# Zero-adding matmuls in TensorE's idle stretches, gate logits by column matmuls, and projections ahead of time in an attention and MLP mix

## The chip, the cores and the metric

The kernel runs on one core of a Trainium2 chip. The metric is device time in microseconds, the median of several runs. TensorE (PE) multiplies, ScalarE (ACT) and VectorE (DVE) work elementwise, GpSimd (POOL) is a slower elementwise engine, and SyncE (SP) issues most DMAs. Each engine takes its own instructions strictly in the order in which they were recorded.

## The reference

Two branches of the same input x (2048 tokens, 512 features, bf16) are mixed by a gate. Attention has 32 heads of 16 features; the other branch is a mixer with two Gelus and two layer norms.

```
x = A_x
g = sigmoid((x * gate_w).sum(-1))
q, k, v = split(x @ wqkv)                  # 32 heads, 16 wide
a = softmax(q k^T / 4) v @ wo
h = gelu(layernorm(x) @ w1)                # 512 wide
hs = shift_tokens(h, by +1, -1, +2, -2 per quarter) @ w2
x1 = x + hs
b = x1 + gelu(layernorm(x1) @ w3) @ w4     # w3: 512 x 1792
out = g * a + (1 - g) * b
```

## The kernel before, in words

**Scores.** Attention goes by rounds: 4 chunks of 512 queries, 4 groups of 8 heads, and two halves of a group, 32 rounds in all. A round has 64 score tiles, each 128 keys by 512 queries of one head: 2048 tiles altogether. A score tile is one matmul (line 800) with 32 rows of the array; up to four run at once in four row strips. Two thirds of the tiles go to ACT, two at a time from a score buffer psA of two PSUM banks (there are two of these), as exact exps (line 880). The others go to DVE, each by way of one of three ring banks: line 906 turns scores into the bits of a number, lines 942 (DVE) and 945 (POOL) make three shifted copies, and the value matmul adds the four up. The value matmuls (line 976) use 17 columns, 16 values and the sum of weights, four heads side by side in the one PSUM bank acc. At a round's end DVE copies acc out (line 992), DMAs and POOL normalise the heads (lines 995 to 1016), with the gate's factor gpk already in it.

**Projections and MLP.** The other products on TensorE are groups of matmuls into a ring bank, four column strips of 32 at once (line 502): q, k and v projections, w1, w2, w3, w4 and the output projection wo. Each is a generator with a planned place `at` (in score tiles issued so far) and a due place. DVE or ACT takes the bank away. There is one Gelu pass for the first MLP (line 693, after w1) and one for each of the four chunks of the second (line 724, between w3 and w4). A pass keeps ACT from its exps, and two loads of its function table lie around it.

**The gate** (lines 598 to 628): sixty-four matmuls, 16 token tiles by 4 pieces of the features, each with 128 x 128 values of x as weights and one column of gate_w moving (line 603). Token logits come out with tokens on partitions; DVE clips them (608), ACT takes the exp, omg = 1 / (1 + exp) is made, and a transpose and DMAs (616 to 627) bring the exps into gpk.

**The order of the work** is made while the program is built. A model of the engines (class Sim) with a cost for each instruction runs through the kernel; whenever it finds TensorE free it calls pe_pick (lines 1129 to 1206). That takes ACT score tiles if a psA buffer is free, DVE tiles if ring banks are free and fewer than DVE_WAIT await DVE, and else, up to the time of the next exp's end, projections (do_gen, from gen_ready) and value matmuls (do_pv). If there is nothing it returns False and TensorE is left idle. All that was emitted is sorted by the model's time and recorded (line 1210). On the chip each engine keeps that order, with semaphores between engines. So a changed constant moves many instructions, and one of TensorE that waits holds back all behind it.

**The end** (lines 1216 to 1262) is written by hand. ACT copies acc; TensorE adds the known part of the last chunk's output projection (`known`, two head groups for each of four token tiles), turns the sums of weights round (line 1237), adds y, the finished other branch (`add_y`), broadcasts the reciprocals (1245) and does the last head group (1255). The four output tiles leave by SP and ACT in turn.

**The start.** Eight zero matmuls (line 480, 512 wide) run while the first inputs load.

Of the kernel before, what the change touches and what calls it, by code (L numbers as in the profile page):

```python
# [233 lines left out]
def kernel(  # L234
# [14 lines left out]
    nc = tc.nc  # L249
# [19 lines left out]
    DVE_STOP = 6  # L269
    DVE_STOP_L = 8  # L270
    URG = 5
    URG_L = 16
    GP3 = 1.0
    DVE_ALONE = 2
    SL = (45, 60)
    IDLE_NS = 544
    FLUSH = 1
    PD_LOW = 0
    PA_LOW = 0
    DVE_WAIT = 2  # L280
    DVE_CAP = 144
    AHEAD = 9
    AHEAD2 = 9
    PV_FULL = 0.92
    PV_IDLE = 0.4
    PRESS = 27
# [7 lines left out]
    P_K = (90, 15)  # L294
    P_V = (8, 6, 6)
    P_V2 = (135, 167)
# [24 lines left out]
    V2 = const.tile([P, NT // 2, H, DH + 1], BF16, name="V2")  # L321
    gw = const.tile([P, KT], BF16, name="gw")
    zero = const.tile([P, 512], BF16, name="zero")
    idb = const.tile([P, P], BF16, name="idb")
# [48 lines left out]
    def dve(hold, deps, fn, **kw):  # L373
        return sim.add(Job("DVE", hold, 150.0, deps, fn, **kw))
# [9 lines left out]

    PSUM_NS = 600.0


# [7 lines left out]
    def W(name):  # L395
        return wb[name].slot
# [41 lines left out]
    dl_w["v1"] = start("SP", 2500.0, col(W("v"), 2 * D + 256, 3 * D))  # L438
    dl_w["g"] = start("SP", 3000.0, lambda q: q.dma_start(out=gw[:], in_=gate_w.rearrange("(kt p) -> p kt", p=P)))
    j_x += [j_x0, j_x1] + [[start("SP", 2500.0, lambda q, c=c: q.dma_start(out=x_sb[:, 4 * c:4 * c + 4, :],  # L440
# [37 lines left out]
    def warm_pe():  # L478
        for _ in range(8):
            nc.tensor.matmul(sim_ring[RING - 1][:], lhsT=zero[:, 0:P], rhs=zero[:], start=True, stop=True)  # L480

# [116 lines left out]
    def gate(at):  # L598
        g = gen("z", at, [dl_w["g"]] + [j_xT[c, 0, k] for c in range(NCH) for k in range(KT)], [])
        units = []  # L600
        for t in range(NT):
            for k in range(KT):
                units.append([Op("full", None, lambda t=t, k=k: nc.tensor.matmul(
                    g.buf.slot[:, t:t + 1], lhsT=W(f"x{t // 4}0")[:, k, (t % 4) * P:(t % 4 + 1) * P], rhs=gw[:, k:k + 1], start=(k == 0),
                    stop=(k == KT - 1)), ns=56.0, name="z")])
        g.units, g.ops = [[o for u in units[i:i + 8] for o in u] for i in range(0, 64, 8)], [o for u in units for o in u]
        g.ops[-1].frees += [wb[f"x{c}0"] for c in range(NCH)]
        e = sim.add(Job("DVE", 120, 150.0, g.ops, lambda: nc.vector.tensor_scalar(
            out=zc[:], in0=g.buf.slot[:, 0:NT], scalar1=60.0, scalar2=-60.0, op0=ALU.min, op1=ALU.max), prio=2,
            frees=[g.buf]))  # L610
        a = act(110, [e], lambda: nc.scalar.activation(out=zE[:], in_=zc[:], func=ACT.Exp))
# [484 lines left out]
    def gen_ready():  # L1096
        if cur_gen[0] is not None:
            return cur_gen[0]
        if not sim.free["ring"]:
            return None  # L1100
        best = None
        for g in gens:
            if g.at <= sim.tiles and (best is None or g.due < best.due) and all(d.done is not None for d in g.deps):
                best = g
        return best
# [23 lines left out]
    def pe_pick():  # L1129
# [71 lines left out]
        if not ops and any(cnt):  # L1201
            do_pv(0.01 if flush else PV_IDLE)
        if not ops:
            return False
        sim.pe_run(ops)
        return True

    sim.run(pe_pick, lambda: acc_round[0] == NR and sim.pending == 0)

    sim.order.sort(key=lambda x: (x[0], x[1]))  # L1210
    if report is not None:
        report.append((sim, [sum(x) for x in n_dve]))
    for _, _, fn in sim.order:
        fn()

# [9 lines left out]
    def known(tt):  # L1225
        for G in range(LG, 4):
            into(tt, lambda a, b: oDbuf[c, G].slot[:, tt * P + a:tt * P + b], lambda: wo[:, G, :], G == LG, False)
# [3 lines left out]

    c = NCH - 1
    nc.scalar.copy(out=ab[:], in_=acc[:])
    known(0)
    known(1)
    for b in range(4):
        nc.tensor.matmul(pd[:, 4 * b:4 * b + 4], lhsT=ab[:, b * P:(b + 1) * P], rhs=idf[:, 0:P:32], start=True, stop=True)
    known(2)
    known(3)
    add_y(1)  # L1240
# [10 lines left out]
    for tt in range(4):  # L1251
        t = NT - 4 + tt
        o = (sim.free["ot"] + sim.free["xn"])[tt]
        for j in range(4):
            nc.tensor.matmul(bank[tt][32 * j:32 * j + 32, :], lhsT=oT[:, tt * P + 32 * j:tt * P + 32 * j + 32], rhs=woL[:],
                             start=False, stop=True, tile_position=(0, 32 * j), skip_group_check=True)
        if tt % 2:
            nc.scalar.activation(out=o[:], in_=bank[tt], func=ACT.Copy, scale=omg[:, t:t + 1])
        else:
            nc.vector.scalar_tensor_tensor(out=o[:], in0=bank[tt], scalar=omg[:, t:t + 1], in1=y_of(tt), op0=ALU.mult,  # L1260
                                           op1=ALU.add)
        (nc.scalar if tt % 2 else nc.sync).dma_start(out=out_flat[t * P:(t + 1) * P, :], in_=o[:])

# [28 lines left out]
```

## Time and profile before

| what | number |
|---|---|
| median of 7 runs | 795.58 us (795.23 to 798.81) |
| the profiled execution's own time | 798.81 us |
| its span, first to last instruction | 797.0 us |
| mean granted TensorE clock | 0.983 |
| exps of ACT, L880 | 737, 1038 ns each, 691.4 us |
| DVE's first step, L906 | 574, 681 ns each, 377.4 us |
| DVE's shifts, L942 | 587, 444 ns mean, 237.7 us |
| POOL's shifts, L945 | 274, 1054 ns each, 288.7 us |
| Gelu passes, L693 and L724 | 7.03 us once, 6.18 us four times; table loads of 1.28 us before and after |

The page gives the busy time of each engine and rows of ten slices' digits, among them PEclk, the share of full clock that TensorE was granted. Matmuls overlap, so a busy TensorE is not one at its peak: four matmuls in four strips run together. "Idle before" in a row of instructions is the time in which that engine stood still ahead of them, with what ended it.

### The profile page before, as it was taken

What the parts mean: (1) busy time and instruction counts of PE and PEld (TensorE: products, weight loads), DVE (VectorE), ACT (ScalarE), POOL (GpSimd) and SP (SyncE); (2) the same over time, 40 slices, a digit from 0 to 9 for tenths busy, and PEclk for the clock granted to TensorE, in tenths of its full rate; (3) what the DMA queues carried; (4) which work ended last, traced back from release to release, by engine and by line L of the source; (5) the groups of instructions that cost most, each with busy time, mean ns of one, the idle gap of its engine ahead of it and who ended that gap; (6) DMA issues with size and microseconds to landing.
All of it is one profiled execution on the core that took longest, in us unless ns stands there. A gap on an engine that the chain in (4) does not pass through costs nothing.

```text
span 797.0 us, 23724 instructions
## 1 busy us (share of the span) xinstructions
PE 766.8 (96%) x9580; PEld 222.8 (28%) x9580; DVE 743.2 (93%) x1589; ACT 742.2 (93%) x763; POOL 342.4 (43%) x335
## 2 busy tenths in 40 slices
PE   9999999999899999969999999999999999998997
PEld 4333322222222222212223222222222222222222
DVE  6999999999999999999998998899998989999994
ACT  6999999999999999999997999999999999999995
POOL 2243445344534445344444444444444444344451
PEclk9989999999999999979999998999999999999999
DMA  9323112122000110343000011101100000000000
GB/s 205 118 56 72 34 35 70 46 67 89 17 10 16 56 34 20 84 132 74 23 23 21 21 29 35 30 20 35 31 19 19 23 27 29 11 19 19 16 20 32
DMA packets 64983, 34.60 MB, mean 43 GB/s; under 512 B 44637, under 2 KB 60269, under 8 KB 64873
## 3 DMA queue, kind: packets, MB, share of 16 engines
q1 hardware_dynamic: 63256, 32.29, 15.7%
q8 instruction: 75, 1.23, 0.6%
q10 hardware_dynamic: 1616, 0.79, 0.4%
q14 instruction: 36, 0.29, 0.1%
HBM read 17.39 MB, written 6.81 MB: 30 GB/s over the span
## 4 chain that ended last, share of the span: by engine, by line
PE 53%; DVE 29%; ACT 9%; issue 4%; DMA 3%; SPq 1%; POOL 1%; ACTq 0%; POOLq 0%; DVEq 0%
PE acc L976 18%; PE ring L502 17%; PE psA L800 16%; DVE PD L906 11%; DVE PD L942 10%; ACT PA L880 6%; ACT hT L724 2%; DMA pk<-den 1%; DVE x_sb L702 1%; DVE st L633 1%; ACT hT L693 1%; PE ring L800 1%; DVE accsb L992 1%; DVE xn L653 1%; DMA x_sb<-in_A_x_dram 1%
## 5 line engine op out<-in xcount | busy, mean ns | idle before, releaser
L880 ACT ACTIVATE PA<-psA 128x1024 bf16<-128x1024 f32 x737 | 691.4, 1038 | 40.5 <-PE psA L800 14.8
L945 POOL TENSOR_SCALAR PD<-PD 128x1024 uint16<-128x1024 uint16 x274 | 288.7, 1054 | 418.3 <-DVE PD L942 290.5
L906 DVE TENSOR_SCALAR PD<-ring 128x512 uint16<-128x512 f32 x574 | 377.4, 681 | 25.2 <-PE ring L800 23.3
L976 PE MATMUL acc<-PD,V 128*17 128x512 bf16 x2296 | 305.4, 384 | 11.9 <-POOL PD L945 6.0
L800 PE MATMUL psA<-q,kT 32*128 32x512 bf16 x1474 | 283.9, 389 | 8.1 <-ACT PA L880 7.8
L976 PE MATMUL acc<-PA,V 128*17 128x512 bf16 x1474 | 268.1, 384 | 0.4 <-ACT PA L880 0.4
L942 DVE TENSOR_SCALAR PD<-PD 128x1024 uint16<-128x1024 uint16 x587 | 237.7, 444 | 2.2
L800 PE MATMUL ring<-q,kT 32*128 32x512 bf16 x574 | 194.0, 390 | 0.9 <-DVE PD L906 0.7
L800 PEld LDWEIGHTS <-kT 32*128 32x128 bf16 x2048 | 72.6, 91 | 309.4 <-issue 308.5
L976 PEld LDWEIGHTS <-V 128*17 128x17 bf16 x3770 | 75.4, 88 | 148.8 <-issue 124.0
L502 PE MATMUL ring<-xnT,w 128*32 128x512 bf16 x1152 | 93.9, 383 | 1.5 <-DVE PD L906 1.0
L502 PE MATMUL ring<-w,hT 128*32 128x512 bf16 x1152 | 93.9, 389 | 0.3 <-DVE qf L571 0.2
L502 PEld LDWEIGHTS <-w 128*32 128x32 bf16 x1920 | 42.8, 95 | 52.9 <-issue 40.7
L502 PE MATMUL ring<-w,w 128*32 128x256 bf16 (+1 forms) x768 | 42.3, 313 | 0.0
L1009 POOL TENSOR_TENSOR oT<-accsb,bcs 128x512 bf16<-128x512 f32 x31 | 40.1, 1293 | 3.2 <-DMA bcs<-rr 2.6
L723 DVE CAST hT<-ring 128x512 bf16<-128x512 f32 x56 | 38.2, 683 | 0.5 <-PE ring L502 0.2
L502 PEld LDWEIGHTS <-hT 128*32 128x32 bf16 x1152 | 24.1, 96 | 34.5 <-issue 26.7
L724 ACT ACTIVATE hT<-hT 128x7168 bf16<-128x7168 bf16 x4 | 24.7, 6177 | 0.0
L992 DVE COPY accsb<-acc 128x512 f32<-128x512 f32 x31 | 21.1, 681 | 1.0 <-PE acc L976 0.9
L633 DVE BATCH_NORM_STATS2 st<-x_sb 128x6 f32<-128x512 bf16 x32 | 21.6, 682 | 0.0
L502 PE MATMUL ring<-w,wq 128*32 128x512 bf16 x256 | 19.9, 383 | 1.1 <-DVE PD L906 0.8
L502 PE MATMUL ring<-wo,oD 128*32 128x512 bf16 x224 | 19.1, 382 | 0.0
(86 smaller groups left out, 202.3 us busy)
## 6 DMA issues: line engine op xcount, KB each, us to landing
bcs<-rr SPq DMA_DIRECT2D x124, 64.0 KB
xn_dram<-xn SPq DMA_DIRECT2D x32, 128.0 KB
w<-in_B_w_dram SPq DMA_DIRECT2D x5, 512.0 KB
oD<-oT SPq DMA_DIRECT2D x124, 16.0 KB
w<-in_B_w_dram SPq DMA_DIRECT2D x4, 448.0 KB
out_dram<-ot SPq DMA_DIRECT2D x13, 128.0 KB
x_sb<-in_A_x_dram SPq DMA_DIRECT2D x3, 512.0 KB
w<-in_A_wqkv_dram SPq DMA_DIRECT2D x2, 256.0 KB
```

Of the source, the lines that this page charges most:

```text
L502: units.append([Op("col", j, lambda j=j, lf=lf, rf=rf, n0=n0, n1=n1, st=st, sp=sp: nc.tensor.matmul(get()[32 * j:32 * j + 32, n0:n1], lhsT ...
L633: a = dve(600, deps, lambda: nc.vector.bn_stats(out=sb.slot[:], in_=x_sb[:, t, :]), prio=6, at=at, acq=[sb])
L723: pre.append(evac(g, PSUM_NS, lambda ps, m=m: nc.vector.tensor_copy(out=h2[:, m, :], in_=ps[:])))
L724: ge = act(93 + 427 * FT + 2600, pre, lambda: nc.scalar.activation(out=h2, in_=h2, func=ACT.Gelu_apprx_tanh), prio=0)
L800: o = Op("row", i, lambda: nc.tensor.matmul(dst(), lhsT=kT[G][32 * i:32 * i + 32, kt * P:(kt + 1) * P], rhs=qbuf[G, c].slot[32 * i:32 * i ...
L880: job = act(hold, ops, lambda: nc.scalar.activation(out=pb.slot[:, 0:n], in_=buf.slot[:, 0:n], func=ACT.Exp, scale=0.25), acq=[pb], frees= ...
L906: nc.vector.tensor_scalar(out=pr["buf"].slot[:, h * 512:(h + 1) * 512], in0=buf.slot[:], scalar1=BITS_MUL, scalar2=BITS_ADD, op0=ALU.mult, ...
L942: nc.vector.tensor_scalar(out=d[k][:, 0:w], in0=d[0][:, 0:w], scalar1=float(SHIFT * k), scalar2=None, op0=ALU.add)
L945: nc.gpsimd.tensor_scalar(out=d[k][:, 0:w], in0=d[0 if both else 2][:, 0:w], scalar1=1.0, scalar2=float(SHIFT * (k if both else 1)), op0=A ...
L976: o = Op("col", i, lambda: nc.tensor.matmul(acc[32 * i:32 * i + DH + 1, :], lhsT=lhs(), rhs=rhs(), start=st, stop=True, tile_position=(0, ...
L992: e = dve(PSUM_NS, round_ops[r], lambda: nc.vector.tensor_copy(out=ab.slot[:], in_=acc[:]), acq=[ab], prio=0)
L1009: n = gp(1250, d3, lambda: nc.gpsimd.tensor_tensor(out=ob.slot[:], in0=ab.slot[:], in1=bb.slot[:], op=ALU.mult), acq=[ob], frees=[ab, bb], ...
```

## The change

There are four parts, and constants that go with them.

- **Filler.** Where pe_pick found nothing to do, it now calls `filler`. From score tile 64 on, if the running round has begun its value matmuls, TensorE has been idle for FILL = 250 ns in the model and no exp ends within 400 ns, it issues a group of four matmuls, 17 columns and 384 wide, of zeros with zeros, that add to acc; and further groups while there is nothing else, at most 60.
- **Gate.** gate_w lies in the first of 32 columns of a zeroed weight tile gwz. Sixteen column matmuls (four pieces of the features by four chunks of 512 tokens) give logits along the free axis on partitions 0, 32, 64, 96; DVE copies the bank to SBUF, and four fp32 matmuls turn them round, as line 1237 does with the sums of weights.
- **Projections ahead.** While ACT is taken for over 1500 ns more (a Gelu pass), generators planned up to EARLY = 68 tiles later may be taken.
- **The end.** known(0) and known(1) are recorded just ahead of the last value matmuls, known(2) and known(3) under ACT's copy of acc; the second output tile leaves by SP instead of ACT.

```diff
-    DVE_STOP_L = 8
+    DVE_STOP_L = 9
-    URG_L = 16
+    URG_L = 18
-    DVE_ALONE = 2
+    DVE_ALONE = 1
+    EARLY = 68
+    FILL = 250
-    FLUSH = 1
+    FLUSH = 2
-    DVE_WAIT = 2
-    DVE_CAP = 144
+    DVE_WAIT = 3
+    DVE_CAP = 140
-    PV_FULL = 0.92
-    PV_IDLE = 0.4
+    PV_FULL = 0.916
+    PV_IDLE = 0.37
-    P_V = (8, 6, 6)
+    P_V = (7, 6, 6)
-    gw = const.tile([P, KT], BF16, name="gw")
-    zero = const.tile([P, 512], BF16, name="zero")
+    gwz = const.tile([P, KT, 32], BF16, name="gwz")
+    zero = const.tile([P, 384], BF16, name="zero")
...
+    nc.gpsimd.memset(gwz[:], 0.0)
+    dl_w["g"] = start("SP", 3000.0, lambda q: q.dma_start(out=gwz[:, :, 0], in_=gate_w.rearrange("(kt p) -> p kt", p=P)))
...
-            nc.tensor.matmul(sim_ring[RING - 1][:], lhsT=zero[:, 0:P], rhs=zero[:], start=True, stop=True)
+            nc.tensor.matmul(sim_ring[RING - 1][:, 0:384], lhsT=zero[:, 0:P], rhs=zero[:], start=True, stop=True)
...
+        g.units = [[Op("col", j, lambda j=j, k=k: nc.tensor.matmul(
+            g.buf.slot[32 * j:32 * j + 32, :], lhsT=gwz[:, k, :], rhs=W(f"x{j}0")[:, k, :], start=(k == 0),
+            stop=(k == KT - 1), tile_position=(0, 32 * j), skip_group_check=True), ns=N_COL, name="z") for j in range(4)]
+            for k in range(KT)]
...
+        zl = Buf("bcs", 1)
+        ez = dve(PSUM_NS, g.units[-1], lambda: nc.vector.tensor_copy(out=zl.slot[:], in_=g.buf.slot[:]), prio=2, acq=[zl],
+                 frees=[g.buf])
+        g2 = gen("z", at, [ez, j_idf], [])
+        g2.units = [[Op("full", None, lambda b=b: nc.tensor.matmul(
+            g2.buf.slot[:, 4 * b:4 * b + 4], lhsT=zl.slot[:, b * P:(b + 1) * P], rhs=idf[:, 0:P:32], start=True, stop=True),
+            ns=200.0, name="z") for b in range(4)]]
...
+        ahead = EARLY if sim.t_free["ACT"] - sim.t > 1500.0 else 0
         for g in gens:
-            if g.at <= sim.tiles and (best is None or g.due < best.due) and all(d.done is not None for d in g.deps):
+            if g.at <= sim.tiles + ahead and (best is None or g.due < best.due) and all(d.done is not None for d in g.deps):
...
         if not ops:
-            return False
+            return filler(tr)
...
+        if sim.tiles < 64 or acc_round[0] == NR or tr is not None and tr - t < 400.0:
+            return False
+        if acc_ready[0] is None or acc_ready[0].done is None or not pv_issued[acc_round[0]][0]:
+            return False
+        if fill["epoch"] != e:
+            if t - e < FILL:
...
+        fill["n"] += 1
+        if fill["n"] > 60:
+            return False
+        r = acc_round[0]
+        ops = [Op("col", i, lambda i=i: nc.tensor.matmul(acc[32 * i:32 * i + DH + 1, 0:384], lhsT=zero[:, 0:DH + 1], rhs=zero[:],
+                                                       start=False, stop=True, tile_position=(0, 32 * i),
+                                                       skip_group_check=True), ns=162.0, name="fill") for i in range(4) if pv_issued[r][i]]
...
+    tl = max(t for t, _, name, _ in sim.pelog if name == "pv")
+    tl = min(t for t, _, name, _ in sim.pelog if name == "pv" and t > tl - 250.0)
+    sim.emit(tl - 1.0, lambda: (known(0), known(1)))
...
     nc.scalar.copy(out=ab[:], in_=acc[:])
-    known(0)
-    known(1)
+    known(2)
+    known(3)
     for b in range(4):
         nc.tensor.matmul(pd[:, 4 * b:4 * b + 4], lhsT=ab[:, b * P:(b + 1) * P], rhs=idf[:, 0:P:32], start=True, stop=True)
-    known(2)
-    known(3)
...
-        (nc.scalar if tt % 2 else nc.sync).dma_start(out=out_flat[t * P:(t + 1) * P, :], in_=o[:])
+        (nc.scalar if tt == 3 else nc.sync).dma_start(out=out_flat[t * P:(t + 1) * P, :], in_=o[:])
```

The recorded program has 265 more matmuls (each fp32 one counted once): 300 of filler, 16 + 4 in place of the gate's 64, and 9 more value matmuls, since 577 score tiles instead of 574 go to DVE.

## The prediction

> **What bounds the kernel now.** I read the page first: the busy shares, the clock row and the chain.
>
> ```profile
> PE 766.8 (96%) x9580; PEld 222.8 (28%) x9580; DVE 743.2 (93%) x1589; ACT 742.2 (93%) x763; POOL 342.4 (43%) x335
> PEclk9989999999999999979999998999999999999999
> PE 53%; DVE 29%; ACT 9%; issue 4%; DMA 3%; SPq 1%; POOL 1%; ACTq 0%; POOLq 0%; DVEq 0%
> ```
>
> Three engines stand above 90%, so which of them decides must be asked stage by stage, by the busy time of each engine in chosen stretches (us, length, then PE, PEld, DVE, ACT, POOL, clock, DMA share, GB/s).
>
> ```profile
> 225.00:340.00 115.00, 113.60 (x1367) 31.05 (x1359) 115.00 (x255) 111.10 (x121) 49.32 (x47) 1.00 0.16 41
> 362.00:480.00 118.00, 115.53 (x1472) 32.51 (x1470) 111.77 (x230) 108.70 (x116) 53.35 (x50) 1.00 0.13 31
> ```
>
> Between the first and the second Gelu pass VectorE is the bound (115.00 of 115). From 362 us on VectorE and ScalarE have 5 to 8% of slack and TensorE has little; in 496 to 605 us it is busy 109.00 of 109. TensorE is the bound of the second half, so its time counts there.
>
> The clock row has dips. The same view, cut to them:
>
> ```profile
> 46.40:53.10 6.70, 6.70 (x81) 2.25 (x80) 6.01 (x18) 5.61 (x8) 2.08 (x3) 0.50 0.35 101
> 354.00:360.20 6.20, 6.13 (x36) 0.97 (x35) 4.22 (x9) 4.92 (x6) 2.09 (x2) 0.50 0.45 110
> 486.54:493.40 6.86, 6.84 (x46) 1.27 (x44) 6.13 (x11) 5.88 (x7) 4.17 (x4) 0.50 0.05 12
> 612.84:616.30 3.46, 3.46 (x29) 1.00 (x31) 1.96 (x5) 3.08 (x3) 1.75 (x2) 0.51 0.00 0
> ```
>
> The first dip follows the 64 gate matmuls (44.39 to 48.64 us). The others follow three of the five Gelu passes, in which ScalarE feeds TensorE no exps for 8.8 us. At clock 0.50 TensorE is busy throughout while DVE and ACT wait. The 3.4 us ahead of each drop (the fourth row: ahead of no drop):
>
> ```profile
> 350.00:353.40 3.40, 0.00 (x0) 0.00 (x0) 3.37 (x12) 3.37 (x3) 0.97 (x2) 0.50 0.50 159
> 483.13:486.54 3.41, 2.06 (x16) 0.65 (x13) 3.34 (x8) 3.39 (x2) 1.88 (x2) 1.00 0.16 48
> 609.43:612.84 3.41, 2.08 (x12) 0.64 (x13) 3.17 (x8) 3.39 (x2) 1.04 (x1) 1.00 0.00 0
> 726.00:729.40 3.40, 2.56 (x20) 0.56 (x15) 2.48 (x6) 3.40 (x1) 2.29 (x2) 1.00 0.00 0
> ```
>
> Twelve or sixteen matmuls in 3.4 us went with a drop; twenty did not.
>
> **The change part by part.** The sum is made on the profiled execution, 798.81 us (span 797.0, 1.8 around it). It is the highest of seven runs; the gain is taken off their median, 795.58.
>
> *Filler.* The changed program's order has 300 zero matmuls, all in the five Gelu passes: 60, 100, 48, 52, 40. In the trace a group of four 512-wide column matmuls starts every 0.216 us (432.46 to 433.54, six groups), so a group of four 384-wide ones takes 0.162 by width, and 75 groups 12.2 us. TensorE's idle time in the passes was 1.79 + 5.70 + 1.86 + 1.73 + 1.76 = 12.8 us. It fits, at full clock; TensorE is the cover, and each group can hold back a real matmul by at most 0.16. At the end of a pass both score buffers stand filled (four exps run without a gap from 353.00), so I cost it at nothing. In the third pass 48 matmuls over 8.77 us are 19 more per 3.4 us: 35 instead of 16, well above the 20 that kept the clock. That zeros count as activity is shown by the warm-up: zero matmuls alone from 1.19 us, 0.427 apart, and the transposes from 4.58 already at full rate (219 ns each).
>
> What a dip costs, from below: the idle time of ACT and DVE in it, as lost score tiles. A pair of tiles costs ACT 1.038, DVE 2 x 0.681 + 2 x 0.444 = 2.25; together 0.963 + 0.444 = 1.41 pairs per us. The three Gelu dips show ACT idle 1.28, 0.98, 0.38 and DVE 1.98, 0.73, 1.50: (1.23+0.88)/1.41 = 1.5, 0.9 and 0.7, sum 3.1. From above, if TensorE alone decides: half its busy time in them, 3.07 + 3.42 + 1.73 = 8.2. The stretches behind them are TensorE's, so the backlog is mostly paid later: I take 6.0.
>
> Here a rule is to be weighed. The Trainium skill ("TensorE: Matmul & The Clock Gate", HAM oscillation) says that the clock drops after idle gaps above some 3.4 us. By it only the second pass (nothing from 349.5 to 354.07) would drop, the third, whose longest gap is 0.8, would not, and the filler would be worth one dip, at most 3.1. The rows show drops at 486.5 and 612.8 without such a gap, so I follow them and count three. By the rule the whole sum below would end near 791.
>
> *Gate.* Sixty-four one-column matmuls stood in four bursts of 0.68, 0.73, 0.30 and 0.30: 2.0 us. In their place are sixteen 512-wide ones (4 x 0.216 = 0.86) and four fp32 ones like L1237 (0.98): 1.8, no difference. Added are a PSUM copy on DVE (0.68) and one more hop. The fp32 matmuls wait for that copy, and all scores behind them on TensorE would wait too; they stand nine tiles after the column matmuls, about 3.5 us at 797/2048 a tile, so between 0 and 0.68, taken 0. The row to zE_dram comes at tile 103 instead of 118, so the four gpk DMAs are earlier; L1000 waited 0.5 for them, gain 0 to 0.5, taken 0. The staging buffer is one of the two that bcs uses; the order puts its release before the first bcs load. The dip goes: by idle time (1.05 + 0.31)/1.41 = 1.0, by half of TensorE's 6.70 us 3.35. The stretch behind it (60 to 200 us: PE 98%, DVE 97%, ACT 96%) is not TensorE's alone: 1.2.
>
> *Projections ahead.* Of the q projections only two really move, from tiles 967 and 1334 into passes 2 and 3 (927, 1249); that of pass 1 lay inside already. Each is 16 matmuls: 4 x 0.216 and a change of mode of some 0.1, 0.96; together 1.9 off TensorE's path. Their evacuations (0.68 + 2 x 0.41 on DVE) move too, into passes where DVE is busy 8.73 of 8.77 and 8.15 of 8.77, and there DVE's tiles fall behind by that. Bounds 0 and 1.9, taken 1.2.
>
> *The split, by the new constants.* ACT's tiles go from 1474 to 1471, DVE's from 574 to 577: ACT -1.6; DVE +2.04, two full and three half shifts +1.6, copy 0.68: +4.3; POOL one shift of 1.05; TensorE 9 more value matmuls, 9/4 x 0.216 = 0.5. The three DVE tiles fall in the first nine heads' rounds (156 for 153), where DVE is full. Cost 0 to 1.8 net there, taken 0.5; TensorE's 0.5 in its half, 0.3. That constants reorder everything else I hold at +-2.
>
> *The tail.* The chain at the end, in order of time (start, us, what):
>
> ```profile
> 786.46 1.00 PE ring L1222 x16
> 787.46 0.98 PE psA L1237 x8
> 788.44 0.55 PE ring L1222 x8
> 788.99 0.43 PE psA L1222 x8
> 789.42 0.86 PE ring L1222 x8
> 790.28 0.88 PE psA L1245 x32
> ```
>
> Sixteen output matmuls go ahead of the last value matmuls, and the other sixteen under the ACT copy (786.54 to 787.12). Then L1237's successor is followed by 0.86 of adding y and, rdl being ready at 789.01, by L1245: 0.86 earlier. One output DMA issue leaves ACT, so the last ACT pass no longer waits 0.44 behind it; on SP it stands behind the first tile's issue and ahead of the third's, which leaves 0.36 later but still earlier than the last. The early sixteen need oD, whose last DMA is issued at 783.1 and takes 2.0 (such a row of the chain: 178.30, 2.02), so 785.1 to 785.7; TensorE is there from 785.3, with the last three value matmuls and the whole tail behind it: 0 to 0.4, taken 0.2. Sum 1.1.
>
> *Start.* The warm-up is eight times 384 wide at 0.320 instead of 0.427: it ends at 3.8 instead of 4.6. The transposes' data is there at 4.3, so 0.3 may be won; a clock released one window later would cost about 1.7 (3.4 us at half). Taken 0. The memset of gwz is first on POOL (0.20, the row of L462); idb is then ready at 1.5, needed at 4.3. The gate's DMA issues at 16.1 on SP, long after the memset, so nothing behind it waits.
>
> Sum: 6.0 + 1.2 + 1.2 + 1.1 - 0.5 - 0.3 = 8.7. In the profiled execution 790.1; on the median **786.9**.
>
> **The rivals.** *The clock is not held* (0.14). Zeros weigh too little in mixed passes, or the 0.25 us gaps the planner leaves ahead of each fill let the clock fall at the same places. Then gate 1.2, projections 1.2, tail 1.1, less 0.8: 2.7, so 792.9. For it: the drops came at a TensorE busy share of 0.61, not of zero. Against: the warm-up, and 35 matmuls for 16.
>
> *Slower: the filler overruns the passes* (0.16). If the clock falls inside passes 2 to 4 anyway, their 50 groups take 0.324 each, 16.2 us in 5.70 + 1.86 + 1.73 = 9.3 of idle time. The 6.9 over stands in TensorE's order ahead of real scores, with the dips still there: 6.9 - 2.7 = 4.2 slower, 799.8. It decides from an overrun of 2.7 us, some 17 groups at half rate beyond the idle time. Against it: fill begins within the first microsecond of a pass, at full clock.
>
> *TensorE decides everywhere* (inside the main case's range): gate 2.0, dips 8.2, projections 1.9, tail 1.5, no costs: 13.6, 782.0.
>
> **How the numbers follow.** Main case 0.70, from 780.5 (the last sum, with 1.5 of the constants' 2) to 791.5; the unheld clock 0.14, 791.5 to 795; slower 0.16, 797 to 802. A measurement here tells about 0.2%, 1.6 us: below 794.0 lie the main case and half of the second (0.76), within are the rest of it (0.08), above the overrun (0.16). The range 780.5 to 795.5 leaves out the overrun and a little below.
>
> **What would show it.** The filler: clock 1.00 through all five passes and after the gate; in the 9 us behind passes 2 to 4 matmuls of 0.38 us, not 0.60, and DVE's waits for TensorE there gone. The projections: ACT idle less than 5% behind passes 2 and 3. The tail: from the last value matmul to the end about 9.7 us instead of 10.9. The gate: no 0.50 at 46 to 53 us. I am wrong if the clock row still dips behind the Gelu passes, if fill matmuls last 0.5 us or more, if the clock in the first 10 us is half, or if DVE's busy share rises to 100% in the second half, so that TensorE's saved time buys nothing.

## The result, and the profile after

The changed kernel takes 791.88 us (median of 14 runs, 790.23 to 794.87), the kernel before 796.37 on the same chip (35 runs): a ratio of 0.9943, 95% interval 0.9930 to 0.9955, so 4.5 us less where 8.7 were forecast. The sign and the range held; the size was half. The profiled execution of the changed kernel took 793.49 us (span 791.7).

The page of the changed kernel: busy time by engine, the granted clock in 40 slices, and the chain that ended last by engine.

```profile
PE 774.4 (98%) x9849; PEld 235.1 (30%) x9849; DVE 748.9 (95%) x1598; ACT 740.3 (94%) x762; POOL 343.2 (43%) x337
...
PEclk9999999999999999999999999999999999999999
...
PE 61%; DVE 31%; issue 3%; DMA 2%; ACT 2%; SPq 1%; POOL 0%; DVEq 0%; ACTq 0%
```

The clock row has no digit below 9 any more. That alone says little, since a slice is 20 us long and a short dip leaves it at 9; the stretches below say more. TensorE and VectorE now hold 92% of the chain (82% before). Its groups (busy us, mean ns of one, then the idle time before them and what ended it):

```profile
L892 ACT ACTIVATE PA<-psA 128x1024 bf16<-128x1024 f32 x736 | 689.5, 1040 | 35.5 <-PE psA L812 18.5
...
L918 DVE TENSOR_SCALAR PD<-ring 128x512 uint16<-128x512 f32 x577 | 377.1, 680 | 13.4 <-PE ring L812 11.9
...
L1242 PE MATMUL acc<-zero 128*17 128x384 bf16 x300 | 20.9, 327 | 0.0
```

The first two before the change:

```profile
L880 ACT ACTIVATE PA<-psA 128x1024 bf16<-128x1024 f32 x737 | 691.4, 1038 | 40.5 <-PE psA L800 14.8
...
L906 DVE TENSOR_SCALAR PD<-ring 128x512 uint16<-128x512 f32 x574 | 377.4, 681 | 25.2 <-PE ring L800 23.3
```

VectorE's idle time ahead of its first steps fell from 25.2 to 13.4 us, of which 11.9 (23.3 before) waited for TensorE. ScalarE's, ahead of its exps, fell only from 40.5 to 35.5. The nine microseconds behind passes 2 to 4, each of which had a dip in the prediction's profile (columns as there), are at full clock with TensorE busy throughout:

```profile
364.00:373.00 9.00, 9.00 (x119) 2.36 (x117) 9.00 (x22) 9.00 (x11) 4.42 (x4) 1.00 0.45 119
486.00:495.00 9.00, 9.00 (x106) 2.50 (x108) 8.38 (x17) 8.92 (x10) 4.44 (x5) 1.00 0.03 7
608.00:617.00 9.00, 9.00 (x112) 2.51 (x112) 9.00 (x20) 8.87 (x11) 4.89 (x6) 1.00 0.01 2
```

In the first of them the matmuls of one form take 384 ns, as forecast, not the 600 of the dip:

```profile
L812 PE MATMUL psA<-q,kT 32*128 32x512 bf16 x20 | 3.9, 384 | 0.0
L506 PE MATMUL ring<-w,hT 128*32 128x512 bf16 x48 | 3.5, 384 | 0.0
```

In the dip of the kernel before (354 to 360.2 us):

```profile
L800 PE MATMUL psA<-q,kT 32*128 32x512 bf16 x10 | 3.0, 601 | 4.6 <-ACT PA L880 4.6
```

One dip is new, at 204.44 to 207.86 us; it begins just ahead of the first Gelu pass and lies mostly in it. In the stretches ahead of it and with it, the first row has two matmuls in 1.80 us:

```profile
201.70:203.50 1.80, 0.12 (x2) 0.09 (x1) 1.80 (x3) 1.80 (x2) 1.36 (x2) 1.00 0.00 0
203.50:207.90 4.40, 4.38 (x44) 1.17 (x47) 3.63 (x7) 4.37 (x3) 1.62 (x2) 0.61 0.04 7
```

and the waits of 200 to 206 us name what TensorE stood for: at the change of a round TensorE's value matmuls wait for VectorE's copy of the accumulator, which no filler bridges, since it adds to that same accumulator.

```profile
PE acc L988 <- DVE accsb L1004: 1.7, 1, 1.7
```

A second profile of the changed kernel (e15 below) has the same wait of 1.7 us there and no dip.

### The profile page after: what moved, and what is told of

Same layout as the page of the kernel before. It is cut to its first block, busy times and chain, and to the rows that moved or that the text cites. A ratio compares the mean times of both kernels' runs of the same rounds, so it can differ in the third digit from the quotient of the medians.

```text
span 791.7 us, 24272 instructions
## 1 busy us (share of the span) xinstructions
PE 774.4 (98%) x9849; PEld 235.1 (30%) x9849; DVE 748.9 (95%) x1598; ACT 740.3 (94%) x762; POOL 343.2 (43%) x337
## 4 chain that ended last, share of the span: by engine, by line
PE 61%; DVE 31%; issue 3%; DMA 2%; ACT 2%; SPq 1%; POOL 0%; DVEq 0%; ACTq 0%
PE acc L988 21%; PE ring L506 20%; PE psA L812 18%; DVE PD L918 12%; DVE PD L954 9%; DVE st L645 1%; DVE xn L665 1%; DMA pk<-den 1%; PE ring L812 1%; DVE x_sb L714 1%; DVE accsb L1004 1%; ACT hT L736 1%; DMA x_sb<-in_A_x_dram 1%; DVE q L577 1%; DVE hT L735 1%
## 5 line engine op out<-in xcount | busy, mean ns | idle before, releaser
L892 ACT ACTIVATE PA<-psA 128x1024 bf16<-128x1024 f32 x736 | 689.5, 1040 | 35.5 <-PE psA L812 18.5
L918 DVE TENSOR_SCALAR PD<-ring 128x512 uint16<-128x512 f32 x577 | 377.1, 680 | 13.4 <-PE ring L812 11.9
L988 PE MATMUL acc<-PD,V 128*17 128x512 bf16 x2308 | 309.0, 382 | 2.9 <-DVE PD L954 2.5
L812 PE MATMUL psA<-q,kT 32*128 32x512 bf16 x1471 | 279.4, 384 | 1.5 <-ACT PA L892 1.2
L954 DVE TENSOR_SCALAR PD<-PD 128x1024 uint16<-128x1024 uint16 (+1 forms) x592 | 240.1, 447 | 2.7
L812 PE MATMUL ring<-q,kT 32*128 32x512 bf16 x577 | 189.1, 384 | 1.2 <-DVE PD L918 1.1
L988 PEld LDWEIGHTS <-V 128*17 128x17 bf16 x3779 | 78.4, 88 | 140.9 <-issue 116.2
L1242 PE MATMUL acc<-zero 128*17 128x384 bf16 x300 | 20.9, 327 | 0.0
```

Source lines behind the costliest of these rows:

```text
L812: o = Op("row", i, lambda: nc.tensor.matmul(dst(), lhsT=kT[G][32 * i:32 * i + 32, kt * P:(kt + 1) * P], rhs=qbuf[G, c].slot[32 * i:32 * i ...
L892: job = act(hold, ops, lambda: nc.scalar.activation(out=pb.slot[:, 0:n], in_=buf.slot[:, 0:n], func=ACT.Exp, scale=0.25), acq=[pb], frees= ...
L918: nc.vector.tensor_scalar(out=pr["buf"].slot[:, h * 512:(h + 1) * 512], in0=buf.slot[:], scalar1=BITS_MUL, scalar2=BITS_ADD, op0=ALU.mult, ...
L954: nc.vector.tensor_scalar(out=d[k][:, 0:w], in0=d[0][:, 0:w], scalar1=float(SHIFT * k), scalar2=None, op0=ALU.add)
L988: o = Op("col", i, lambda: nc.tensor.matmul(acc[32 * i:32 * i + DH + 1, :], lhsT=lhs(), rhs=rhs(), start=st, stop=True, tile_position=(0, ...
```

## The experiments

Eighteen runs followed, each beside the kernel before on the same chip (its median there was 796.1 to 796.6; e16 to e19 are single executions, beside one of 795.34). "Us at half clock" is worked out from each run's mean clock c and span: 2 (1 - c) x span, the median over its runs; for the kernel before it is 17 to 19, and for the changed kernel 3. (The clock is recorded to 0.001, which is 1.6 us.)

| run | us, median | ratio to before, interval | us at half clock |
|---|---|---|---|
| changed kernel | 791.88 | 0.9943, 0.9930 to 0.9955 | 3 |
| changed kernel again (e15) | 792.30 | 0.9951, 0.9936 to 0.9967 | 1 |
| changed, no fill, same order (e1) | 795.50 | 0.9979, 0.9961 to 0.9996 | 13 |
| changed, longer warm-up (e2) | 792.69 | 0.9947, 0.9928 to 0.9966 | 2 |
| changed, fill twice (e9) | 797.83 | 1.0030, 1.0010 to 1.0050 | 2 |
| changed, half the fill (e11) | 793.71 | 0.9961, 0.9946 to 0.9975 | 1 |
| changed, narrow fill (e12) | 793.31 | 0.9960, 0.9948 to 0.9973 | 5 |
| changed, EARLY = 0, planned anew (e8) | 800.59 | 1.0047, 1.0030 to 1.0063 | 2 |
| before, new tail (e4) | 795.73 | 0.9991, 0.9975 to 1.0008 | 17 |
| before, fill in the passes, same order (e5) | 794.78 | 0.9978, 0.9963 to 0.9993 | 8 |
| before, new gate, same order (e10) | 797.07 | 1.0008, 0.9995 to 1.0021 | 17 |
| before, fill, gate, tail, same order (e13) | 795.91 | 0.9994, 0.9986 to 1.0003 | 8 |
| the same, clock held at the gate (e14) | 795.72 | 0.9995, 0.9982 to 1.0009 | 4 |
| before, new gate, planned anew (e6) | 816.93 | 1.0263, 1.0237 to 1.0289 | 41 |
| before, new plan only (e7) | 816.82 | 1.0256, 1.0233 to 1.0280 | 34 |

**The filler, in both orders.** The theory was the prediction's (A: a held clock is worth 5 to 6 us), the rival that a dip is cheap (B). The first kernel keeps the changed order and leaves the zero matmuls out:

```diff
-        ops = [Op("col", i, lambda i=i: nc.tensor.matmul(acc[32 * i:32 * i + DH + 1, 0:384], ...
+        ops = [Op("col", i, lambda i=i: None, ns=162.0, name="fill") for i in range(4) if pv_issued[r][i]]
```

> The changed kernel with its 300 zero matmuls left out and every other instruction in the same order on every engine. Theory A (the prediction's): the clock held through the Gelu passes is worth about 6 us, so without it the time is some 5 to 6 us above the changed kernel's 791.9, near 797 to 798, with the clock at 0.50 for 3 to 10 us behind passes 2 to 4. Theory B (a dip is cheap: the score buffers and copies ahead of it are worked off while TensorE is slow, and the engines that bound the stages around it catch up): the dips come back, but the time is only 0.5 to 2.5 us above, 792.5 to 794.5.

The second keeps the order of before and issues 304 zero matmuls where its plan leaves TensorE idle in and just behind the passes:

```diff
+    passes = [(t, t + h) for e, t, h, _ in sim.log if e == "ACT" and h > 5000.0]
...
+        if end > 0.0 and any(a < end and s < z + 1400.0 for a, z in passes):
+            t = end + 120.0
+            while t + 230.0 < s:
+                for i in range(4):
+                    sim.emit(t + i, lambda i=i: nc.tensor.matmul(
+                        acc[32 * i:32 * i + DH + 1, 0:384], lhsT=zero[:, 0:DH + 1], rhs=zero[:, 0:384], start=False,
...
```

> The kernel before, its order on every engine unchanged, with 304 zero matmuls put into TensorE's planned gaps in and just behind the five Gelu passes. Theory A: no dips behind passes 2 to 4 and about 5 to 6 us less than before, near 791. Theory B: no dips, but only 0.5 to 2.5 us less, 794 to 796. If the zero matmuls stand in the way of real ones, it is no faster or slower than before.

Measured: without its fill the changed order takes 795.50, so the fill is worth 3.6 us there by the medians, 2.9 by the ratios (0.9979 against 0.9943); in the old order it is worth 1.7. By the intervals of the ratios that is 1.2 to 4.6 in the changed order and 0.6 to 2.9 in the old: B, or something between, and not A. The clock behaved as wanted in both: e5 kept only the gate's dip.

**The warm-up and the tail.** Eleven warm-up matmuls of 384 instead of eight; and the new tail alone in the kernel before.

```diff
-        for _ in range(8):
+        for _ in range(11):
```

> The changed kernel with eleven warm-up matmuls 384 wide instead of eight, as long as the eight 512-wide ones before. In the trace of the changed kernel the first transposes and projections run at half rate until 9.9 us and the first score matmul starts at 12.3 us instead of 10.9. If the shorter warm-up is the cause, the first score matmul is back at 10.9 and the whole is 1.4 us shorter, near 790.5; if the start is made good later by other slack, the first score is at 10.9 but the time stays within 0.5 of 791.9. Both theories A and B expect the former.

> The kernel before with the changed end alone (sixteen output matmuls ahead of the last value matmuls, sixteen under the copy of acc, the second output tile on the SP queue); all else as before. The prediction's working gives 0.86 + 0.44 less 0.2 = 1.1 us less than before, 795.3 for 796.4. If the early sixteen hold back the last value matmuls while oD lands, it is 0.5 us less or nothing.

The longer warm-up brought the first score matmul from 12.3 to 11.1 us in its profile, but its median is not told apart from the changed kernel's. The tail gave 0.7 us, with an interval that holds zero; its profile shows 0.7 us less from the last score matmul to the end (12.0 for 12.7 to 12.8).

**Single parts, planned anew.** Three kernels take one part of the change and let the planner order everything again: the new gate in the kernel before, the new constants with EARLY in the kernel before, and the changed kernel with EARLY = 0.

> The kernel before with the new gate alone (16 column matmuls of 512, PSUM copy, four fp32 matmuls), its warm-up cut into 11 pieces of 384 so that it is as long as before; old constants, old tail, no filler. The dip at 47 to 54 us (6.8 us at half clock) should be gone, those behind the Gelu passes stay. Theory C (each us at half clock costs 0.30, the slope over all runs of the kernel before so far; the gate's instructions themselves cost nothing): -2.0, so 794.4. Theory of the prediction: -1.2, so 795.2. Rival (the new gate's extra hop and the PSUM copy cost what the dip gave): 0, 796.4.

> The kernel before with the new constants of the planner and the projections ahead alone; no filler, old gate, old tail. Theory C (the clock explains the whole gain): no change, 796.4, as many us at half clock as before. Theory of the prediction: projections 1.2 less constants 0.8, so -0.4 +-2, 796.0. Rival (the plan is worth what the prediction lacks or more, and the clock less): -2 or beyond, 794.4 or below.

> The changed kernel with EARLY = 0: the order is planned anew without projections ahead of time, everything else stays, the fill included (316 matmuls). Theory of the prediction: projections ahead are worth 1.2, so this is slower than the changed kernel by 1.2, 793.1. Theory C: they are worth nothing, 791.9, within 0.5.

All theories missed by far: 20.6, 20.5 and 8.7 us slower than the kernel each was made from. The row of e6 for 90 to 100 us says why it can't be read as the price of a gate:

```profile
90.00:100.00 10.00, 10.00 (x148) 3.95 (x142) 8.18 (x18) 0.73 (x1) 0.00 (x0) 0.73 0.11 19
```

ScalarE has one instruction in 10 us there, because the new plan piled projections and value matmuls in front of its scores. That is a plan's accident, not the edit's cost. In e8 the clock is 0.999, and its loss lies in many stretches, the end among them (14.1 us from the last score matmul on, for 12.3). What EARLY alone is worth therefore stays open; from here on orders were kept.

**The fill's own price.** In the changed order: every zero matmul twice; every second group left out; 192 columns instead of 384.

```diff
+            nc.tensor.matmul(acc[32 * i:32 * i + DH + 1, 0:384], lhsT=zero[:, 0:DH + 1], rhs=zero[:],
+                                                       start=False, stop=True, tile_position=(0, 32 * i),
```

> The changed kernel in the same order, every zero matmul issued twice (600 for 300). Prediction's reason (TensorE is idle there and the passes cover the fill): the first 12.2 us of fill filled the 12.8 us of idle time, so the second 12.2 us stand over; at full clock and with ScalarE in the passes for 8.8 us each, between 0 and +4 taken as TensorE being late at each pass's end by up to 2.4 us. If fill has a price already in the changed kernel (theory D: it stands ahead of real matmuls), twice the fill costs the same amount again and more: +2 to +6, with VectorE waiting for TensorE in the passes. If TensorE has slack there: 0 to +1.

> The changed kernel in its own order with every second group of zero matmuls left out (about 150 of 300). Twice the fill cost 5.9 us for 12.2 us of matmuls, 0.49 per us. If that price holds from the first fill on (theory D) and the clock stays held, half the fill is faster by up to 3.0: 789. If the first 300 lie in idle time (the prediction) and the clock stays held: 791.9 +-0.5. If half the fill doesn't hold the clock: dips behind some passes, up to 13.5 us at half clock, 793 to 795.5.

> The changed kernel in its own order with zero matmuls 192 wide instead of 384, as many of them (6.1 us instead of 12.2 by width). Theory D (fill costs 0.49 per us): 789 if the clock is held. The prediction (fill lies in idle time): 791.9 +-0.5 if held. If what keeps the clock is TensorE's busy share and not the number of matmuls, dips come back: 793 to 795.5.

Twice the fill costs 5.9 us by the medians (6.9 by the ratios) for 12.2 us more of matmuls, about half a us per us. The pass of the changed kernel, and of the one with twice the fill, over the same 16 us:

```profile
355.20:371.00 15.80, 14.96 (x226) 6.60 (x222) 15.66 (x38) 15.77 (x12) 7.51 (x7) 1.00 0.50 134
```

```profile
354.10:370.00 15.90, 15.90 (x287) 8.63 (x281) 13.58 (x30) 13.27 (x9) 5.99 (x6) 1.00 0.49 116
```

With 300 zeros TensorE still has 0.84 us idle and ScalarE none; with 600 TensorE is full and ScalarE waits 2.6 us, VectorE 2.3. So the first 300 fit, as the prediction held, and the next do not. Half the fill and the narrow fill are not faster, so theory D (a price from the first fill on) falls. Half the fill kept the clock as well as the whole, yet it took 793.71 where 791.9 +-0.5 was expected; its interval overlaps that of the changed kernel, so whether this is a loss stays open. The narrow fill lost the clock once behind pass 2, at 364.8 us:

```profile
361.40:364.80 3.40, 2.08 (x26) 0.58 (x28) 3.37 (x11) 3.39 (x4) 0.39 (x2) 1.00 0.40 97
364.80:368.20 3.40, 3.40 (x32) 0.62 (x34) 2.22 (x6) 2.37 (x3) 2.27 (x2) 0.50 0.66 196
```

**The gate, in the old order.** The 16 column matmuls are issued in four groups at the places of the 64 old ones, with the PSUM copy behind the last and the four fp32 matmuls ahead of the clip:

```diff
+        def column(n):
+            if n % 16 == 0:
+                for j in range(4):
+                    nc.tensor.matmul(g.buf.slot[32 * j:32 * j + 32, :], lhsT=gwz[:, n // 16, :],
...
-                units.append([Op("full", None, lambda t=t, k=k: nc.tensor.matmul(
...
+        units = [[Op("full", None, lambda n=n: column(n), ns=56.0, name="z")] for n in range(NT * KT)]
```

> The kernel before in its own order, nothing planned anew, with the new gate put into the old gate's places (16 column matmuls in four groups, PSUM copy, four fp32 matmuls ahead of the clip; warm-up as 11 pieces of 384). The dip behind the gate goes if the column matmuls keep the clock. Theory C (0.30 us for each us at half clock): 6.8 us less of it, -2.0, 794.4. The prediction's price for it: -1.2, 795.2. Rival (the wait of TensorE for the PSUM copy, up to 0.7, and the switches of mode eat it): -0.5 to 0, 796.

The dip moved from 46 to 50 us and stayed 6.8 us long. The new gate doesn't hold the clock by itself: at the old places TensorE is fed too little ahead of it.

```profile
46.90:50.40 3.50, 2.54 (x21) 0.85 (x20) 3.50 (x10) 3.50 (x5) 0.00 (x0) 1.00 0.45 150
50.40:57.20 6.80, 6.80 (x48) 2.67 (x48) 4.46 (x11) 2.99 (x5) 3.35 (x4) 0.50 0.35 80
```

**All but the plan.** The order of before with fill, gate and tail (e13); then also nine groups of zero matmuls between the gate's groups (e14); and the changed kernel again beside it.

> The kernel before in its own order with everything of the change that needs no new plan: the zero matmuls in the passes (304), the new gate in the old gate's places, the new tail. The clock should be held throughout. Theory C (only the clock and the tail matter, the new plan is worth nothing): before at no dip 790.4 to 791.2, tail -0.7, fill's own price 1.3 as the same fill showed with the gate's dip left: 791.0 to 791.8, the same as the changed kernel. Rival P (the new plan is worth the prediction's projections less split, 0.4 or more): 792.3 or above. Rival Q (the new plan costs): 790 or below.

It took 795.91 us, and the gate's dip stayed (49.4 to 56.2 us), so the clock was not held as expected. The groups between the gate's:

```diff
+            if n % 4 == 0 and n % 16 and n < 48:
+                for j in range(4):
+                    nc.tensor.matmul(g.buf.slot[32 * j:32 * j + 32, 0:384], lhsT=zero[:, 0:32], rhs=zero[:], start=False,
```

> The kernel before in its own order with zero matmuls in the passes, the new tail and the new gate in the old gate's places, and now nine groups of zero matmuls (four of 384 each) between the gate's groups, where TensorE was fed only 21 matmuls in 3.4 us and dropped. The clock should be held at the gate too, so all of the change is in it but the new plan. From the run without these groups (795.9, 7.1 us at half clock): 0.30 each, -2.1, 793.8. Theory C (the new plan is worth nothing): the same as the changed kernel on this chip, within 1. Rival P (the new plan is worth 1 to 3): the changed kernel is ahead by that.

> The changed kernel once more, as it is, beside the run before on the same chip, since its distance to the order of before is wanted to 1 us and the medians of the kernel before differed by 0.3 between chips. Theory C: 792, no difference to the kernel beside it (within 1). Rival P: 791.5 to 792.5 while the other stands at 793.8 or above.

In e14's profile the clock is held everywhere (46.00 to 56.00 us below), and yet its median is 795.72, against 792.30 for the changed kernel on the same chip: rival P's outcome, a plan worth 3.4 us by the medians (1.9 to 5.1 by the intervals of the ratios). Over all its runs e14 still has 4 us at half clock in the median, but that is little of the difference: its three executions with a mean clock of 1.000 took 794.55 to 795.07, the four such of the changed kernel beside it 790.64 to 793.58, on the average 3.0 less.

```profile
46.00:49.50 3.50, 3.30 (x44) 1.27 (x41) 3.50 (x9) 3.27 (x5) 0.43 (x1) 1.00 0.43 143
49.50:56.00 6.50, 6.35 (x79) 2.51 (x76) 6.00 (x16) 5.54 (x8) 3.35 (x4) 1.00 0.32 67
```

My theory C, that the clock alone explains the 4.5 us, rested on a slope: over 95 runs of the kernel before, each us at half clock goes with 0.31 us of time (standard error 0.03; chip by chip 0.16 to 0.46), and 0.31 x 16 is 4.9. e14 refutes it: fill, gate, tail and a clock almost held bought 0.4 us in the old order (from 1.4 gained to 0.7 lost by the interval), where the tail alone had shown 0.7. A slope over runs of one kernel is not the price of a dip.

**More profiles of the orders without fill.** Since the order of a kernel is fixed, more profiles of it show what varies between executions. The kernel before twice more, the changed one without fill twice more:

> The kernel before as it is, a second profile: the one at hand is of a slow execution (27.3 us at half clock against 18 to 19 in the median). Same order, so by tiles of scores the stretches without a dip should take the same time to 0.3 us; the total should differ by the dips' 0.2 to 0.3 us each and by the start. If instead stretches without a dip differ by more, the clock is not what varies and the slope over runs (0.30) is no price.

> The changed kernel without its zero matmuls in the same order, a second profile: the first was of an execution of 793.0 while the median is 795.5. Theory (dips are what varies): this one shows other or longer dips, each us at half clock 0.2 to 0.3 longer than the same stretch of the changed kernel. Rival: it starts later, first scores at 12 us or more instead of 10.7.

> The kernel before, a third profile, for the same comparison: stretches without a dip alike to 0.3 us; which dips come varies.

> The changed kernel without its zero matmuls, a third profile, for the same comparison: either more time at half clock than 17 us or a later start explains the 2.5 us between the first profile and the median.

The table gives the time between the starts of the score matmuls of two tiles, read from the traces, with the us at half clock in it in brackets; "start" is the first score matmul, "end" from the last one to the end of the span.

| profile | start | 0 to 896 | 896 to 1120 (pass 2) | 1120 to 1376 (pass 3) | 1376 to 1696 (pass 4) | 1696 to 2047 | end |
|---|---|---|---|---|---|---|---|
| before, of the prediction | 10.9 | 330.6 (6.8) | 92.4 (10.2) | 98.9 (6.8) | 119.2 (3.4) | 132.3 | 12.7 |
| before, e16 | 10.9 | 330.1 (6.8) | 91.2 (6.8) | 97.0 | 119.3 (3.4) | 132.2 | 12.8 |
| before, e18 | 11.0 | 330.1 (3.4) | 92.4 (10.2) | 97.0 | 118.9 | 132.4 | 12.8 |
| before + fill, e5 | 10.8 | 333.0 (6.8) | 90.3 | 97.0 | 118.4 | 132.1 | 12.8 |
| before, clock held, e14 | 11.1 | 332.3 | 90.3 | 97.0 | 118.4 | 132.1 | 12.0 |
| changed, no fill, e1 | 10.7 | 330.5 (3.4) | 89.1 (6.8) | 95.7 | 121.5 (6.8) | 131.3 | 12.4 |
| changed, no fill, e17 | 12.5 | 332.9 (3.4) | 89.1 (3.4) | 95.6 | 120.2 (3.4) | 131.3 | 12.4 |
| changed, no fill, e19 | 12.3 | 333.2 (3.4) | 89.1 (3.4) | 95.6 | 121.4 (6.8) | 131.3 | 12.3 |
| changed | 12.3 | 332.2 (3.4) | 89.0 | 95.7 | 119.1 | 131.3 | 12.3 |
| changed again, e15 | 12.3 | 332.3 | 88.9 | 95.7 | 119.0 | 131.3 | 12.3 |

From tile 1120 on, stretches of one order without a dip mostly agree to 0.1 us; the widest scatter is in the stretch of pass 4, 118.4 to 118.9 in the old order and 119.0 to 119.9 in the changed one (119.9 in e2, whose clock is held). In pass 2 they don't quite agree (90.3 in e5 and e14, 91.7 in e13, none with a dip), and up to tile 896 they scatter by 3 us with and without fill. So a dip's price can be read behind passes 3 and 4: in the old order 1.9 for 6.8 us (one profile) and 0.8 to 0.9 for 3.4, some 0.25 per us; in the changed order at most 2.4 for 6.8 and 1.1 for 3.4, some 0.34, and less by 0.9 against e2's 119.9. Behind pass 2 it is 2.1 for 10.2 and 0.9 for 6.8 in the old order, each less by up to 1.4 if e13 is the measure, and nothing in the changed one.

The traces offer a reason for that nothing. The dips of e17 and e19 in pass 2 lie wholly inside the pass, and of e1's 6.8 us all but 1.1: there ScalarE has no exps to do, and a slow TensorE holds up little. The narrow fill's dip (e12) lies wholly behind pass 2, in the same order, and its 3.4 us cost 1.3 to 1.4 (90.3 for 88.9). Behind pass 4 the part of a dip that lay behind ScalarE's first exp was 3.0 us in e17 and 5.2 to 5.6 in e1 and e19. So the part of a dip behind the pass is what costs, at most some 0.3 to 0.5 us per us of it.

## Why the size was wrong, step by step

**The dips: the step that failed.** The step is the filler's term, 6.0 us for a held clock. The prediction had "sum 3.1" from below, "8.2" from above, and took 6.0, "the stretches behind them are TensorE's, so the backlog is mostly paid later". Two things were wrong with the 6.0.
First, and the larger, the execution: it counted three Gelu dips with 20.5 us at half clock, and took their price off the median. Two other profiles of the kernel before have 10.2 each; the dip of pass 3 is in neither, nor in e4 or e10, which keep that order. The prediction itself noted that its execution was the highest of seven.
Second, the price: even in that execution the three dips cost 2.1 + 1.9 + 0.8 = 4.8, and nothing of it is paid later (tiles 1696 to 2047 take 132.1 to 132.4 with and without). In e16 and e18 they cost 0.9 + 0.9 = 1.8 and 2.1. So of the 6.0 the price took 1.2 and the execution some 3.
The fill's measured worth agrees with these sums: 1.7 us in the old order (e5). In the changed order the profiles give 2.0 behind pass 4 (121.0, the mean of e1, e17 and e19, to 119.0; 1.1 against e2's 119.9) and nothing elsewhere; the medians 3.6, the ratios 2.9. All fall well short of 6.0.
The rule that the prediction weighed fares worse than it thought. Its first row of "the 3.4 us ahead of each drop", 350.00 to 353.40, already lies in the drop (clock 0.50), which began at 350.01, half a microsecond into the idle stretch of 349.5 to 354.07. In the 3.41 us ahead of it TensorE was busy 1.77 us with 15 matmuls. So none of the three Gelu drops had an idle gap of 3.4 us ahead of it, and counting three was right for that execution.

**The gate** was taken at 1.2. The dip at 46 us is gone in the changed kernel, as forecast, but e10 shows that the gate alone doesn't do it: what stands around it counts, and that the plan set. Between the starts of tiles 64 and 192, read as in the table, the old gate with its dip of 6.8 us took 51.2 to 51.8 (before, e16, e4, e5), the new one at the old places with such a dip 52.5 and 52.3 (e10, e13), and with the clock held 51.1 (e14). So at the old places the new gate costs about 1 us there and the held clock gives about that back. What it is worth at the places of the changed plan is not isolated.

**Projections ahead and the new constants** were taken at +1.2 and -0.8. In the table the new order, clock held, gains against e14 1.3 (tiles 896 to 1120), 1.3 (1120 to 1376) and 0.8 (1696 to 2047), and loses 0.6 (1376 to 1696): 2.8 us in TensorE's half, where the prediction put its gain. With e13's 91.7 for pass 2 it would be 4.2; the medians of e14 and e15 say 3.4. That is more than the 1.2 it was given. Up to tile 896 the changed order is behind: nine profiles of it (the five of the table, e2, e9, e11, e12) have a mean of 332.2 (330.5 to 333.2), eight of the old order (e4, e10, e13 with the five) 331.2 (329.8 to 333.0). The stretch up to that tile, of e15 and then of e18:

```profile
0.00:344.60 344.60, 335.17 (x4203) 105.22 (x4204) 333.33 (x739) 321.41 (x340) 147.43 (x153) 1.00 0.25 64
```

```profile
0.00:341.20 341.20, 331.74 (x4202) 101.17 (x4202) 327.92 (x733) 321.24 (x341) 142.80 (x147) 0.99 0.25 63
```

VectorE, the third busy figure, has six more instructions and 5.4 us more work there; from there to tile 1376 it has 3.3 less than in e5 (173.60 for 176.93). That is the step "cost 0 to 1.8 net there, taken 0.5": right in its place, and about 1 instead of 0.5, though the scatter there is as large. How the plan's gain divides between projections and constants is not shown, since e7 and e8 made plans of their own.

**The tail**, taken at 1.1, gave 0.7 in e4's profile and 0.5 in the changed kernel's from the last score matmul on, and 0.9 from the start of the last value matmul on (10.0 us for 10.9, where 9.7 was forecast). In the chain of the changed kernel (start, us, what) the sixteen early output matmuls come first, and L1289 begins at 784.91, right behind its predecessors:

```profile
780.77 1.00 PE ring L1259 x17
...
782.93 0.99 PE psA L1283 x8
783.91 0.99 PE ring L1259 x8
784.91 0.87 PE psA L1289 x32
785.78 0.86 PE psA L1259 x8
```

**The start**, taken at 0 with 1.7 as its bound, came near the bound in most profiles. In the first 9.9 us of the changed kernel the transposes take 312 ns and the projections behind them 588, half rate:

```profile
L526 PE MATMUL ring<-idb,x_sb 128*128 128x128 bf16 x32 | 3.9, 312 | 0.7 <-DMA x_sb<-in_A_x_dram 0.7
L484 PE MATMUL ring<-zero 128*128 128x384 bf16 x8 | 2.7, 524 | 1.1 <-DVE zero L473 1.1
L506 PE MATMUL ring<-w,w 128*32 128x512 bf16 x16 | 1.7, 588 | 0.0
```

In the kernel before (e16) they take 244 and 382:

```profile
L480 PE MATMUL ring<-zero 128*128 128x512 bf16 x8 | 3.6, 631 | 1.2 <-DVE zero L469 1.2
L522 PE MATMUL ring<-idb,x_sb 128*128 128x128 bf16 x32 | 2.6, 244 | 0.6 <-DMA x_sb<-in_A_x_dram 0.6
...
L502 PE MATMUL ring<-w,w 128*32 128x512 bf16 x16 | 1.0, 382 | 0.0
```

The warm-up of 2.7 us instead of 3.6 let the first scores slip from 10.9 to between 12.3 and 12.5 us in six profiles of nine; in e1's, e8's and e9's they came at 10.7 to 11.3. None of the eleven profiles with a warm-up of 3.6 or 3.7 us starts late. The page's clock row shows 9 there all the same, so the half rate is read from the matmuls alone. What it costs the median is not shown: e2, which starts at 11.1, is no faster, and its profiled execution lies 1.3 us above its median just as the changed kernel's two lie 1.3 and 1.6 above theirs.

Summed over the profiles, from the mean of e16 and e18 to that of the two of the changed kernel: start +1.4, to tile 896 +2.1, then -2.9, -1.3, 0, -1.0, end -0.5. That is -2.2, against -3.8 and -4.5 by the medians of two chips. The two of the changed kernel ran 1.3 to 1.6 above their medians, e16 and e18 some 0.5 below the kernel's, so about half of the gain lies in executions that no profile shows. As an estimate from these figures, of the 4.5 the filler is about 2 to 3.6, the plan's second half most of the rest, the tail 0.5 to 0.7, and the start and VectorE's half take some back. That the total stayed inside the range is in part luck: the filler gave 2 to 4 less than forecast, the plan in TensorE's half some 2 more.

**The forecast's own tests.** Right: clock 1.00 behind the gate and in passes 2 to 5, with one dip at the first; 384 ns behind the passes; fill matmuls of 327 ns; VectorE's waits for TensorE in the nine microseconds behind passes 2 to 4, which fell from 2.0 to 2.1 us each to 0, 0.6 and 0. ScalarE is idle 4.9, 4.7 and 4.1% between passes 2 and 5, below the 5% named, but behind pass 3 it was at 4.7% before too, so this shows little. Of the signs of being wrong one came: the first 10 us ran at half rate. The rivals: the clock is held, so the first falls; an overrun needs more than 300 zeros, and with 600 there is one (e9), at full clock and 1.5 us over the kernel before; TensorE deciding everywhere falls with 13.6.

## What to carry to other kernels

A dip of the clock costs what it delays where it stands, here 0 to 0.4 us per us at half clock, and next to nothing while the engine that TensorE feeds is busy with something else; count dips over several executions before summing them, and don't take the price from a slope over runs. Filler is free only as long as it fits the idle time: 12 us of it fitted here, the next 12 cost about half their length. Where a planner orders everything, a part planned anew is another plan (9 to 21 us of accident for effects of 1 to 3 us): test parts in a fixed order, and compare stretch by stretch, which in TensorE's half mostly repeats to 0.1 us where totals scatter by 3.

## What the runs showed of the hardware

The clock fell where TensorE had been fed little, mostly without an idle gap of the length that the Trainium skill names ("TensorE: Matmul & The Clock Gate", HAM oscillation: gaps above some 3.4 us). Here 2.08 us of 3.40 busy with 26 matmuls came ahead of a drop (e12), 2.54 of 3.50 with 21 too (e10), while the prediction's fourth row, 2.56 of 3.40 with 20, came ahead of none. But neither the busy time in the profile nor the number of matmuls divides the cases. In e16 2.29 us of 3.40 with 20 matmuls (483.2 to 486.6) came ahead of no drop, and ahead of the gate's dip in the kernel before TensorE was busy most of the time:

```profile
42.80:46.20 3.40, 2.87 (x48) 1.24 (x41) 3.40 (x9) 3.34 (x5) 2.05 (x2) 1.00 0.03 5
```

There 25 of the matmuls were the gate's, one column wide, each shown as 163 ns. What the hardware weighs stays open.
Drops last 3.41, 6.83 or 10.24 us. In each of the eleven profiles with more than one, their starts lie whole multiples of 3.413 us apart (before: 89, 129 and 166 of them from the first), and in the same order the same drop starts at 46.22, 46.46 or 49.45 us. That agrees with a window that runs on its own, as that page has it (What's actually happening). It would also explain why one execution holds 27 us of dips and the next 14: the same thin stretch falls otherwise into the windows.
Zero operands hold the clock: with 152 zero matmuls instead of 300 (e11) it was 1.00 from the first pass's fill to the last scores, where the same order without them dropped behind or in passes 2 and 4 (e1, e17, e19).
